# A new table of places for the same 1630 operations of a gated linear attention and channel-mix kernel

## The chip, the cores and the metric

One core of a Trainium2 chip runs the whole program. The metric is the device time of one execution in microseconds (us); lower is better. Engines named below: TensorE (PE; its weight loads are PEld), VectorE (DVE), ScalarE (ACT), GpSimd (POOL), and SyncE, whose queue (SP) issues every load and store.

## The reference

```python
# attention: B=4, H=8, S=768, D=48; per head a complex D x D state with decay a
for t in range(S):
    new_re = ar * S_re - ai * S_im
    new_im = ar * S_im + ai * S_re
    kv = np.einsum('bhd,bhe->bhde', k[:, :, t], v[:, :, t])
    S_re, S_im = (new_re + kv, new_im)
    y[:, :, t] = np.einsum('bhd,bhde->bhe', q[:, :, t], S_re)
...
# channel mix on x = y as (B, S, 384), d_ff = 1024
xk = mu_k * x + (1.0 - mu_k) * x_prev
xr = mu_r * x + (1.0 - mu_r) * x_prev
k = np.maximum(xk @ w_k, 0.0)
v = k * k @ w_v
r = 1.0 / (1.0 + np.exp(-(xr @ w_r)))
return (r * v).astype(np.float32)
```

## The kernel before

The sequence is cut into 8 units of 384 positions (4 batches, two halves each), numbered u. For each unit there are three groups of operations. **gate(u)** loads the four rows a_re, a_im, k, q (`g`), turns the decays into logarithms and angles (ScalarE: Ln, Exp, Arctan, Sin; VectorE: running sums along the positions with `tensor_tensor_scan`) and multiplies k and q by the resulting factors (`times`, L730), so that the recurrence becomes ordinary products. **attend(u)** stacks q by DMA (`stack`), transposes the keys (`tr`, L884 in unit 0 and L821 after), copies them out of PSUM (`kt`, L891/L898 and L830/L834, ScalarE), forms state updates (`up`, L923 and L853), scores (`sc`, L970 and L965) and outputs (`y`, L1011). **mix(u)** forms xk and xr, the products with w_k (called f in the table; tile `z`, L384 in unit 0, L388 after), relu and square on ScalarE (L429, L433), the products with w_v (tile `o`, L469), the products with w_r (also tile `z`), the sigmoid and the store. Unit 0 works in plain float32; from unit 1 on each operand of the mix is split in two parts (`hi`, `lo`) and each product is three passes. The weights come as ten pieces `raw` (`fetch`), are put together (`convert`: a cast on ScalarE, L535, and one VectorE instruction, L540) and later split (`split`, L559 and L562).

ScalarE holds one set of functions at a time. `act` (L248, L255) loads a set whenever the next function in program order is not in the present one: Ln and Exp are in set 6, Arctan and Sin in set 9, Sigmoid in set 2. So the order decides how many loads there are.

What sets the order of everything is the table `ORDER`: for each group (`("g", u)`, `("a", u)`, `("m", u)`, and `f`, `w`, `s` for fetch, convert and split) it gives each operation its place from 0 to 1629. `Plan.run` sorts all operations by place and emits them, and each engine then runs its own ones in that order, waiting for what it needs. SP issues its DMAs in that order too. Matmul results go to a pool of 5 PSUM tiles (`ps`, used by tr, up, sc, y and z alike; `pso` holds o), so a matmul group can wait for a tile until ScalarE or VectorE has emptied an older one.

```python
    def op_act(n, f, psum=False, **kw):
        op(f, **kw)
...
    def op_pe(cost, f, **kw):
        op(f, **kw)
...
        for i in sorted(range(len(order)), key=order.__getitem__):
            emit, after, _ = self.ops[i]
            assert after <= done
            emit()
```

The first arguments of these helpers (an operation's cost) are not read in this file.

Of the kernel before, what the change touches and what calls it, by code (L numbers as in the profile page):

```python
# [22 lines left out]
C = H * D  # L23
# [208 lines left out]
def tile_kernel(ctx, tc, gat, vt, w_all, mu, slow_g, slow_v, out):  # L232
# [29 lines left out]
    def op_act(n, f, psum=False, **kw):  # L262
        op(f, **kw)
# [970 lines left out]
```

## Time and profile before

| what | value |
|---|---|
| median of 3 runs | 428.28 us (428.24 to 428.5) |
| profiled execution, its own time | 429.0 us |
| its span (first to last instruction) | 427.0 us |
| instructions in the span | 13402 |
| TensorE busy | 375.1 us, 88% |
| VectorE busy | 327.9 us, 77% |
| ScalarE busy | 315.9 us, 74% |
| mean granted TensorE clock | 0.965 of full |

The profiled execution took 2.0 us more than its span, and lies 0.72 us above the median. Busy time is the sum of an engine's instructions; a granted clock of 1.00 is TensorE's full 2.4 GHz and 0.50 is 1.2 GHz. A row of the trace that ends in brackets gives the idle time of the engine just before it and what ended that.

### The profile page before, as it was taken

Reading aid. Unit: us, or ns where it says so; the run is one execution under the profiler, and the core shown is the slowest. Engines: PE = TensorE matmul, PEld = TensorE weight load, DVE = VectorE, ACT = ScalarE, POOL = GpSimd, SP = SyncE. Lnnn points to the kernel's source line nnn. Section 1 sums busy time; section 2 is a strip of 40 time slices with the busy share of each in tenths; the row PEclk is TensorE's granted clock in tenths of the full one; section 3 lists DMA queues with packets and bytes.
Section 4 is the critical chain, followed back from the end, with each engine's and each line's share of the span. In section 5 each row is a group of like instructions: output and inputs, shape, how many; then the busy total and the mean of one; then the engine's idle time right before and its main releaser. Section 6 shows DMA issues by size and latency. Waiting matters only on the chain.

```text
span 427.0 us, 13402 instructions
## 1 busy us (share of the span) xinstructions
PE 375.1 (88%) x5705; PEld 336.1 (79%) x5705; DVE 327.9 (77%) x528; ACT 315.9 (74%) x618; POOL 8.7 (2%) x32
## 2 busy tenths in 40 slices
PE   0047758999989999999999999999998999999991
PEld 0036734776679999999899999999997999999991
DVE  4998669889987989988989779879897684263342
ACT  6999599978977899779977896879885733361430
POOL 6000000000000000000000000000000000000000
PEclk9998659999989999999999999999999999999997
DMA  7989450464431333444331572344220340200101
GB/s 280 411 302 256 120 228 2 102 174 178 98 95 46 150 117 84 122 186 124 84 98 44 199 161 64 125 158 97 85 57 6 88 104 20 71 0 2 56 2 64
DMA packets 22996, 49.72 MB, mean 116 GB/s; under 512 B 4848, under 2 KB 16368, under 8 KB 22928
## 3 DMA queue, kind: packets, MB, share of 16 engines
q1 hardware_dynamic: 22928, 48.78, 37.2%
q8 instruction: 47, 0.77, 0.8%
q14 instruction: 21, 0.17, 0.1%
HBM read 31.06 MB, written 4.72 MB: 84 GB/s over the span
## 4 chain that ended last, share of the span: by engine, by line
PE 59%; ACT 25%; DVE 8%; issue 3%; DMA 2%; SPq 1%; ACTq 0%; DVEq 0%
PE z L388 23%; PE o L469 15%; PE y L1011 8%; PE up L853 5%; PE sc L970 3%; ACT L248 3%; ACT r L255 2%; PE z L384 2%; ACT sq L255 2%; PE tr L821 2%; ACT ph L255 2%; DVE ph L695 2%; DVE g L685 2%; ACT r L718 2%; ACT m L255 2%
## 5 line engine op out<-in xcount | busy, mean ns | idle before, releaser
L388 PE MATMUL z<-x,w 128*128 128x384 f32 x693 | 129.8, 340 | 1.0 <-ACT kt L830 1.0
L388 PEld LDWEIGHTS z<-x,w 128*128 128x128 f32 x693 | 119.3, 188 | 2.6 <-ACT kt L830 1.4
L469 PE MATMUL o<-hx,w 128*128 128x384 f32 x504 | 98.4, 342 | 0.0
L469 PEld LDWEIGHTS o<-hx,w 128*128 128x128 f32 x504 | 86.3, 188 | 1.0
L429 ACT ACTIVATE r<-z 128x384 f32<-128x384 f32 x64 | 30.1, 487 | 26.9 <-PE z L388 24.4
L730 DVE TENSOR_TENSOR g<-g,r 128x768 f32<-128x768 f32 (+1 forms) x24 | 41.6, 1754 | 8.8 <-ACT r L255 8.1
L433 ACT ACTIVATE h<-r 128x384 f32<-128x384 f32 x64 | 33.6, 525 | 4.7 <-DMA out_t<-y 3.7
L441 DVE CAST hx<-h 128x384 fp32r<-128x384 f32 x44 | 15.6, 356 | 26.0 <-PE o L469 15.4
L255 ACT ACTIVATE sq<-m 128x1152 f32<-128x1152 f32 (+1 forms) x30 | 28.0, 966 | 6.8 <-DVE m L651 3.1
L445 DVE TENSOR_TENSOR hx<-h,hx 128x384 fp32r<-128x384 f32 x56 | 30.6, 554 | 0.9 <-ACT h L433 0.2
L384 PE MATMUL z<-x,wx 128*128 128x384 f32 x66 | 24.6, 521 | 5.3 <-DVE x L347 5.3
L884 PE MATMUL tr<-ident,g 128*128 128x128 f32 x18 | 4.5, 405 | 28.1 <-DVE stat L704 27.2
L248 ACT ACT_TABLE_LOAD x22 | 28.2, 1283 | 1.2 <-PEq L1223 0.8
L364 DVE TENSOR_TENSOR x<-xm,x 128x384 fp32r<-128x384 f32 x42 | 22.6, 553 | 8.2 <-ACT x L361 7.7
L1011 PEld LDWEIGHTS y<-q,state 112*48 112x48 f32 (+1 forms) x704 | 23.5, 137 | 6.5 <-issue 4.0
L1011 PE MATMUL y<-q,state 112*48 112x64 f32 (+1 forms) x704 | 26.0, 230 | 2.6 <-ACT r L429 1.5
L361 ACT CAST x<-xm 128x384 fp32r<-128x384 f32 x42 | 21.2, 516 | 8.1 <-DVE xm L353 8.1
L853 PEld LDWEIGHTS up<-v,kt 64*64 64x64 f32 (+1 forms) x1216 | 22.5, 132 | 5.9 <-issue 1.7
L970 PEld LDWEIGHTS sc<-g 48*64 48x64 f32 x1200 | 24.2, 143 | 3.6 <-issue 2.0
L970 PE MATMUL sc<-g 48*64 48x64 f32 x1200 | 26.8, 235 | 0.0
L884 PEld LDWEIGHTS tr<-ident,g 128*128 128x128 f32 x18 | 2.9, 203 | 28.6 <-issue 27.2
L853 PE MATMUL up<-v,kt 64*64 64x48 f32 (+1 forms) x1216 | 25.2, 223 | 0.2
(89 smaller groups left out, 589.4 us busy)
## 6 DMA issues: line engine op xcount, KB each, us to landing
g<-in_gat SPq DMA_DIRECT2D x18, 768.0 KB, 5.7
raw<-in_w_all SPq DMA_DIRECT2D x9, 767.8 KB, 9.1
g<-in_gat SPq DMA_DIRECT2D x12, 384.0 KB, 8.1
v<-in_vt SPq DMA_DIRECT2D x24, 192.0 KB, 3.8
out_t<-y SPq DMA_DIRECT2D x24, 192.0 KB, 2.0
q<-g SPq DMA_DIRECT2D x84, 48.0 KB, 2.4
q<-g SPq DMA_DIRECT2D x28, 144.0 KB, 2.9
q<-g SPq DMA_DIRECT2D x40, 72.0 KB, 2.5
```

What stands on the lines that cost most here:

```text
L248: nc.scalar.add_instruction(mybir.InstLoadActFuncSet(name=nc.get_next_instruction_name(), act_func_set_id=n, engine=mybir.EngineType.Activ ...
L255: nc.scalar.activation(out=out, in_=in_, func=func, **kw)
L384: nc.tensor.matmul(z, lhsT=wx[s[0]][:, s[1]], rhs=hi[which][:, ct], start=ct == 0, stop=ct == NT - 1)
L388: nc.tensor.matmul(z, lhsT=wt[s[0]][:, part, s[1]], rhs=r[which][:, ct], start=n == 0, stop=n == 3 * NT - 1)
L429: nc.scalar.activation(out=t["r", j], in_=t["f", j], func=AF.Relu, scale=1.0 / W_SCALE)
L433: nc.scalar.activation(out=t["h", j], in_=t["r", j], func=AF.Square)
L445: nc.vector.tensor_tensor(out=t["lo", j], in0=t["h", j], in1=t["hi", j].bitcast(F32), op=ALU.subtract)
L469: nc.tensor.matmul(tiles["o", mt], lhsT=w, rhs=r, start=j == 0 and n == 0, stop=j == NJ - 1 and n == len(parts) - 1)
L730: nc.vector.tensor_tensor(out=g[:, d, 2 * i:2 * i + 2], in0=g[:, d, 2:4], in1=t["r"][:, 1 - i, d].unsqueeze(2).to_broadcast([P, k, 2, U]), ...
L853: nc.tensor.matmul(t["up", c, s][i * HR:(KR if i else HR), h * D:(h + 1) * D], lhsT=keys, rhs=V[u][c][r, h * D:(h + 1) * D], start=True, s ...
L970: nc.tensor.matmul(y, lhsT=g[:, 2 * i, q], rhs=g[:, 2 * i + 1, q], start=i == 0, stop=i == 1)
L1011: nc.tensor.matmul(t["y", team][s][rows, h // 2 - team[0], c], lhsT=lhsT[:, cols], rhs=rhs, start=(s, h % 2) not in begun, stop=stop)
```

## The change

Nearly every place in `ORDER` is new; no operation is added or taken away. The numbers handed to the helpers as costs change in seven lines as well, and these are not read when the kernel is built. A few lines of the diff:

```diff
 ORDER = {
-    ("g", 0): (0, 2, 1, 10, 13, 19, 4, 3, 23, 7, 9, 12, 15, 17, 22, 25, 27, 11, 14, 18, 21, 20, 28, 32, 37, 39, 40,
...
+    ("g", 0): (0, 1, 2, 35, 3, 6, 10, 56, 5, 7, 9, 14, 18, 11, 12, 17, 20, 15, 19, 24, 26, 22, 25, 29, 32, 42, 34, 23,
...
-        cost = 1.97 if whole else 1.62
+        cost = 1.97 if whole else 1.61
...
-                op_pe(0.1 + 0.82 * m, f0, heat=0.8, reads=k, writes=[("sc", u, team)],
+                op_pe(0.1 + 0.82 * m, f0, heat=0.68, reads=k, writes=[("sc", u, team)],
```

What it moves on the engines, at three places. First ScalarE in the gate of unit 0, in the program's first part (`sq<-m` is Exp or Ln of set 6, `ph<-ph` Arctan and `r<-r` Sin of set 9, L718 an absolute value, L535 a weight cast). Before:

```order
L255 ACTIVATE sq<-m 128x384 x6
L248 ACT_TABLE_LOAD
L255 ACTIVATE ph<-ph 128x384 x3
L535 CAST hx<-raw 128x768 x2
L718 ACTIVATE r<-r 128x384 x2
L255 ACTIVATE r<-r,half_pi 128x384 x2
L255 ACTIVATE r<-r 128x384 x2
L535 CAST hx<-raw 128x768
L718 ACTIVATE r<-r 128x384
L255 ACTIVATE r<-r,half_pi 128x384
L622 ACTIVATE m<-g 128x1152
L255 ACTIVATE r<-r 128x384
```

With the new table the same stretch reads:

```order
L255 ACTIVATE sq<-sq 128x384 x2
L248 ACT_TABLE_LOAD
L255 ACTIVATE ph<-ph 128x384 x3
L535 CAST hx<-raw 128x768
L248 ACT_TABLE_LOAD
L255 ACTIVATE sq<-m 128x384 x4
L718 ACTIVATE r<-r 128x384
L255 ACTIVATE sq<-m 128x384 x2
L535 CAST hx<-raw 128x768
L718 ACTIVATE r<-r 128x384
L248 ACT_TABLE_LOAD
L255 ACTIVATE r<-r,half_pi 128x384
```

The six Exp that feed L685 stood ahead of the Arctan and now stand behind it, so set 9 is loaded, then set 6 again, then set 9 again. Up to the keys' first copy ScalarE issues five loads instead of three; from there on the number is the same in both.

Second TensorE at the start of unit 0's mix (numbers tell tiles apart; an `x3` row of L384 is one product). Before:

```order
L384 MATMUL z_736<-x_717,wx_236 128x384 x3
L384 MATMUL z_749<-x_717,wx_206 128x384 x3
L384 MATMUL z_761<-x_717,wx_306 128x384 x3
L469 MATMUL o_774<-h_769,wx_206 128x384
L469 MATMUL o_776<-h_769,wx_206 128x384
L469 MATMUL o_778<-h_769,wx_206 128x384
L384 MATMUL z_788<-x_746,wx_727 128x384 x2
L384 MATMUL z_788<-x_746,wx_743 128x384
L384 MATMUL z_798<-x_746,wx_727 128x384 x2
L384 MATMUL z_798<-x_746,wx_743 128x384
L821 MATMUL tr_809<-ident_66,g_138 128x128 x3
```

With the new table:

```order
L384 MATMUL z_745<-x_721,wx_309 128x384 x3
L384 MATMUL z_761<-x_721,wx_180 128x384 x3
L384 MATMUL z_768<-x_721,wx_241 128x384 x3
L384 MATMUL z_782<-x_721,wx_326 128x384 x3
L469 MATMUL o_794<-h_777,wx_180 128x384
L469 MATMUL o_796<-h_777,wx_180 128x384
L469 MATMUL o_798<-h_777,wx_180 128x384
L384 MATMUL z_806<-x_757,wx_728 128x384 x2
L384 MATMUL z_806<-x_757,wx_733 128x384
L384 MATMUL z_818<-x_757,wx_728 128x384 x2
L384 MATMUL z_818<-x_757,wx_733 128x384
L821 MATMUL tr_829<-ident_66,g_141 128x128 x3
```

A fourth w_k product now stands ahead of the first group into o, and a fifth between the transposes; the second group into o moved back.

Third TensorE where the mix of unit 0 ends and the attention of unit 2 begins (`o<-h` are the last groups of unit 0, `tr`, `sc`, `up` those of unit 2). Before:

```order
L469 MATMUL o<-h,wx 128x384 x6
L821 MATMUL tr<-ident,g 128x128 x6
L469 MATMUL o<-h,wx 128x384 x3
L821 MATMUL tr<-ident,g 128x128 x3
L970 MATMUL sc<-g 64x64 x48
L821 MATMUL tr<-ident,g 128x128 x6
L853 MATMUL up<-v,kt 64x48 x2
```

With the new table:

```order
L469 MATMUL o<-h,wx 128x384 x3
L821 MATMUL tr<-ident,g 128x128 x6
L469 MATMUL o<-h,wx 128x384 x3
L821 MATMUL tr<-ident,g 128x128 x6
L469 MATMUL o<-h,wx 128x384 x3
L970 MATMUL sc<-g 64x64 x48
L821 MATMUL tr<-ident,g 128x128 x3
L853 MATMUL up<-v,kt 64x48 x2
```

Before, three of unit 2's six groups of transposes (an `x3` each) stand ahead of the scores and two right behind them; now four stand ahead, two by two between groups into o, and one behind. After the first state update the program before has a second one ahead of four mix products of unit 1 (36 matmuls of L388); with the new table those 36 come first.

## Rows read from the trace of the kernel before

**Rows 1.** The page: busy time by engine; granted TensorE clock in 40 slices, tenths.
```profile
PE 375.1 (88%) x5705; PEld 336.1 (79%) x5705; DVE 327.9 (77%) x528; ACT 315.9 (74%) x618; POOL 8.7 (2%) x32
...
PEclk9998659999989999999999999999999999999997
```

**Rows 2.** Stretches of 20 us: length, busy time (instructions) by engine, granted clock, DMA share, GB/s.
```profile
20.00:40.00 20.00, 10.77 (x258) 8.96 (x258) 18.30 (x35) 19.01 (x38) 0.00 (x0) 0.91 0.88 278
...
60.00:80.00 20.00, 18.07 (x146) 10.42 (x145) 17.35 (x23) 19.16 (x30) 0.00 (x0) 0.94 0.29 99
...
100.00:120.00 20.00, 18.36 (x155) 11.49 (x153) 18.60 (x25) 19.44 (x34) 0.00 (x0) 1.00 0.42 119
```

**Rows 3.** TensorE in order of time: start, length, engine, line, operation, count [idle before].
```profile
27.22 0.87 PE L884 MATMUL tr<-ident,g 128*128 128x128 f32 x3 [27.22 <-DVE stat L704]
...
32.95 0.90 PE L923 MATMUL up<-v,kt 64*64 64x48 f32 x48 [0.94 <-ACT kt L891]
...
53.94 0.91 PE L1011 MATMUL y<-pt,v 64*64 64x64 f32 x24
58.96 1.65 PE L384 MATMUL z<-x,wx 128*128 128x384 f32 x2 [4.12 <-DVE x L347]
60.82 6.28 PE L384 MATMUL z<-x,wx 128*128 128x384 f32 x16 [0.21 <-DVE x L347]
67.82 2.20 PE L469 MATMUL o<-h,wx 128*128 128x384 f32 x6 [0.72 <-ACT h L433]
71.01 4.11 PE L384 MATMUL z<-x,wx 128*128 128x384 f32 x12 [0.99 <-DVE x L347]
...
118.91 0.55 PE L821 MATMUL tr<-ident,g 128*128 128x128 f32 x3 [1.10 <-ACT kt L830]
120.19 0.55 PE L821 MATMUL tr<-ident,g 128*128 128x128 f32 x3 [0.74 <-ACT kt L834]
...
123.38 1.43 PE L853 MATMUL up<-v,kt 64*64 64x48 f32 x64
...
124.74 6.51 PE L388 MATMUL z<-x,w 128*128 128x384 f32 x36
...
213.26 3.39 PE L388 MATMUL z<-x,w 128*128 128x384 f32 x18 [1.05 <-ACT kt L830]
...
327.36 1.38 PE L1011 MATMUL y<-q,state 112*64 112x64 f32 x40 [1.46 <-ACT r L429]
```

**Rows 4.** Stretches of 4 us; columns as in the stretches of 20 us.
```profile
48.00:52.00 4.00, 4.00 (x98) 3.68 (x97) 3.02 (x6) 1.90 (x6) 0.00 (x0) 0.50 0.08 20
...
120.00:124.00 4.00, 3.81 (x95) 3.22 (x99) 2.40 (x5) 2.93 (x10) 0.00 (x0) 0.57 0.35 80
```

**Rows 5.** The end of the program in order of time, VectorE.
```profile
417.49 1.49 DVE L486 SCALAR_TENSOR_TENSOR y<-o,zr 128x384 f32<-128x384 f32 x3 [1.64 <-PE o L469]
```

**Rows 6.** ScalarE in order of time, first 60 us.
```profile
18.37 1.28 ACT L248 ACT_TABLE_LOAD   x1
19.66 1.35 ACT L255 ACTIVATE ph<-ph 128x384 f32<-128x384 f32 x3
...
24.07 1.10 ACT L255 ACTIVATE r<-r,half_pi 128x384 f32<-128x384 f32 x2
25.08 0.92 ACT L255 ACTIVATE r<-r 128x384 f32<-128x384 f32 x2
...
26.81 0.51 ACT L718 ACTIVATE r<-r 128x384 f32<-128x384 f32 x1
...
56.36 1.03 ACT L535 CAST hx<-raw 128x768 f16<-128x768 bf16 x1
```

**Rows 7.** VectorE in order of time: unit 0's factors, unit 1's last split.
```profile
27.23 3.56 DVE L730 TENSOR_TENSOR g<-g,r 128x768 f32<-128x768 f32 x4
...
126.42 1.02 DVE L364 TENSOR_TENSOR x<-xm,x 128x384 fp32r<-128x384 f32 x2
```

**Rows 8.** Groups by line and shape: count, busy us, mean ns, idle before with releasers.
```profile
L562 DVE TENSOR_TENSOR w<-wx,w 128x768 fp32r<-128x768 f32 x9 | 8.6, 954 | 0.4 <-ACT w L559 0.4
```

More of the change, by code (lines that the diff above doesn't have):

```diff
@@ L368, in begin @@
                     x = [("X", u, ct), ("X0", u)]
-                    op_act(U, whole_old, reads=x, writes=[("xo", u, which, ct)], uses=[part_slot[which]] + use)
+                    op_act(U + 115, whole_old, reads=x, writes=[("xo", u, which, ct)], uses=[part_slot[which]] + use)
                     op_dve(U + 60, whole_new, reads=[*x, ("xo", u, which, ct)], writes=[("xhi", u, which, ct)],
@@ L544, in convert @@
             r, k = [("raw", i + 1)], [("wx", j) for j in range(s.start, s.stop)]
-            op_act(n * C, f0, reads=r, writes=[("upper", i % HB)], uses=[sx])
+            op_act(n * C + 216, f0, reads=r, writes=[("upper", i % HB)], uses=[sx])
             op_dve(n * C, f1, reads=[*r, ("upper", i % HB)], writes=[*k, ("raw", i)], uses=[sx])
@@ L836, in f2 @@
                             in_=t["tr", c, part].rearrange("p (i j x) -> p j i x", i=NT, j=2)[:, :, :, D:])
-                    op_pe(0.41, f0, heat=0.8, reads=[("kqs" if part else "kqc", u, ct) for ct in range(NT)],
+                    op_pe(0.35, f0, heat=0.8, reads=[("kqs" if part else "kqc", u, ct) for ct in range(NT)],
                           writes=[("tr", u, c, part)], uses=[sp, g_slot[u]])
@@ L854, in up @@
                                                  lhsT=keys, rhs=V[u][c][r, h * D:(h + 1) * D], start=True, stop=True)
-                op_pe(0.535 * len(subs), up, heat=0.8, reads=[("kt", u, c, i) for i in range(4)] + [("v", u, c)],
+                op_pe(1.07, up, heat=0.8, reads=[("kt", u, c, i) for i in range(4)] + [("v", u, c)],
                       writes=[("up", u, c, s) for s in subs], uses=[*su, sk, v_slot[u][c]])
@@ L899, in f2 @@
                                        in_=t["tr", p, part].rearrange("p c (j x) -> p c j x", j=2)[:, :, :, D:])
-                    op_pe(0.41, f0, heat=0.8, reads=[("kqs" if part else "kqc", u, p)],
+                    op_pe(0.35, f0, heat=0.8, reads=[("kqs" if part else "kqc", u, p)],
                           writes=[("tr", u, p, part)], uses=[sp, g_slot[u]])
@@ L1026, in f0 @@
                                 add(h, c, s, V[u][c][r], pt(h)[r, c], c == NC - 1 and h // 2 == team[-1])
-                op_pe(0.2 + (0.19 * len(inter) + 1.05) * m / 2, f0, heat=0.8,
+                op_pe(0.2 + (0.19 * len(inter) + 1.05) * m / 2, f0, heat=0.68,
                       reads=[("pt", u, p, j) for p in team for j in range(2)] + [("v", u, c) for c in range(NC)]
```

232 rows, old and new, of the table ORDER are left out of this document.

## Prediction

> **What bounds the kernel now.** I read the page first. TensorE is busy for 375.1 of 427.0 us, ScalarE and VectorE for 316 and 328 [rows 1], so no engine is full by itself, and the clock line shows two weak places: the fourth to sixth slice (32 to 64 us) and the twelfth. The stretches of 20 us then say where TensorE is idle. Between 20 and 40 us it is busy for 10.8 us while ScalarE is busy for 19.0 [rows 2], and it begins only at 27.22 us [rows 3]. From 60 us on it is nearly full. So the program has two parts. In the first 60 us ScalarE and VectorE, which make the factors of unit 0, set the pace. After that the end is TensorE's own work plus whatever waits stand in it.
>
> Third I went through TensorE in order of time for those waits. The last product of unit 0's attention ends at 53.94 + 0.91 = 54.85 us, the mix's products run from 60.82 on (two start at 58.96), and behind that there are 0.72 and 0.99 us in unit 0's mix, 1.10 and 0.74 us ahead of transposes of unit 2, 1.05 us at 213 and 1.46 us at 327 [rows 3]. That is 6.06 us in all. One more loss is not idle time: between 120 and 124 us the granted clock is 0.57 [rows 4]. A mean of 0.57 between the levels 1.0 and 0.5 is 86% of the time at 1.2 GHz; of 3.81 us busy 3.3 ran at half speed, where 1.6 would have done. The two waits of 1.10 and 0.74 us stand just before, and TensorE was busy only 18.36 of the 20 us up to there [rows 2]. Behind the last matmul the program needs 427.0 − 417.49 = 9.5 us for multiplying, storing and its closing check [rows 5]; the new order leaves that tail alone.
>
> So a new order can win at most these 6.1 + 1.6 us behind 60 us, and whatever moves the start of the mix.
>
> **The start: later.** The new table puts the six Exp behind the Arctan, and ScalarE loads two more sets of functions. One load takes 1.28 us and the next ScalarE instruction starts 0.01 us after it ends [rows 6], so I price two at 2 × 1.285 = 2.57 us. Two Sin and one absolute value now also stand ahead of the Sin that gates the first product of k and q: 0.92 + 0.51 us less than the overlap between neighbours, 1.3 us. It ended at 25.2 us [rows 6]; now it ends at 25.2 + 2.57 + 1.3 = 29.1, or 28.1 if ScalarE's 0.99 us of idle time between 20 and 40 us [rows 2] is used up first. TensorE now starts with the scores, which need both products of VectorE, 3.56 / 4 = 0.89 us each [rows 7]. First matmul: 28.1 + 1.8 = 29.9 to 30.9, against 27.22. The keys' copies come behind the same loads, so the first state update (32.95) moves by 2.6 as well.
>
> What of that reaches the end? The unit's products wait for each other through ScalarE and VectorE, and there are waits to eat into, such as the 0.94 us before the state update [rows 3]. From 48 to 52 us TensorE is 100% busy at a granted 0.50 [rows 4], so the last part of that chain cannot shrink at that clock. I take 1.9 of the 2.57 us as arriving at the last product, 56.75. Behind it the old order has a weight cast of 1.03 us at 56.36 [rows 6] between the outputs' copies and the mix's first operand; in the new one it has gone ahead. So the mix starts at 60.82 + 1.9 − 1.0 = 61.7: **+0.9 us**. Bounds: all of the delay hidden, −1.0; all 3.4 us that the keys can be late (2.57 plus one long Exp's worth of reordering) passed on, +2.4.
>
> **Unit 0's mix: the waits go.** The first group into o waited 0.72 us for the square of a product just made, and the w_r products waited 0.99 us for VectorE's mixing [rows 3]. Now four w_k products instead of three precede it. A product takes some 2.1 us (12 matmuls in 4.11 [rows 3]), and that much time passes on ScalarE and VectorE too. Nothing else is ahead of these two, so both waits vanish: **−1.7** (between 0 and −1.7).
>
> **Unit 2's transposes: the waits and the low clock go.** Three groups stood right around the scores and waited for ScalarE to empty PSUM tiles. Now they stand two by two between groups into o, each about 2 us long, in which ScalarE makes the copies. Without 1.84 us of idle time there I let the clock stay up: 1.84 + 1.6 = **−3.4** (0 if ScalarE is as late as before).
>
> **At 213 and 327 us.** Both waits are for ScalarE to empty a PSUM tile, and both neighbourhoods are ordered anew: **−2.5** (0 to −2.5).
>
> **New waits.** A new order makes its own. The thinnest place that I found is the one where four mix products of unit 1 moved ahead of a state update. They need VectorE's last split, which ended at 126.42 + 1.02 = 127.4 [rows 7]. Nine VectorE instructions that were ahead of it are now behind, among them the last three weight splits at 0.95 us or less [rows 8], and one is new: 4.6 us by their lengths, so 122.8. TensorE would be there at 124.74 − 3.4 − 0.8 (the two terms above) − 1.4 (the update that moved behind, 1.43 at 123.38 [rows 3]) = 119.1. The gap is 3.7 us if VectorE keeps its old times, and under 1 if it moves up as TensorE does, since most of what it waits for is TensorE and ScalarE; I take 1.5. For two more places with a PSUM tile as releaser I take 0.6 each, half of what such waits cost at 213 and 327. Sum **+2.7**, bounds 0.8 and 7.6 (all that was won is given back).
>
> **Sum.** 429.0 (the profiled execution's own time) + 0.9 − 1.7 − 3.4 − 2.5 + 2.7 = 425.0. The three runs' median lies 0.72 below that execution, so I forecast **424.3 us** for the median.
>
> **A rule against the change.** The trace has a load of functions followed at once by the next instruction, 18.37 + 1.28 = 19.65 against 19.66 [rows 6]. The Trainium skill, *ScalarE: Activation LUTs*, section "What ACT_TABLE_LOAD costs", adds a drain of about 1.38 us to each switch and gives about 2.66 us in total; by that page (an estimate) two more loads would cost 5.3 us and the sum would be 2.7 us higher, 427.0. No such drain is to be seen in this row, so I keep 2.57.
>
> **Rivals.** *The start decides (slower).* ScalarE is busy 19.0, 19.2 and 19.4 of 20 us at 20, 60 and 100 us [rows 2]. If that engine and not TensorE carries the first 120 us, its 2.57 us are passed on whole, the two waits in unit 0's mix and those at 119 us stay since they end on ScalarE's copies, and only the later ones can go: 428.3 + 2.57 − 2.5 + 1.2 = 429.6. Against it: ScalarE has 0.8 us idle at 60 to 80 and 0.6 at 100 to 120 us, and at 119 us it is the order of its copies that is late. It decides if the mix starts after 64 us.
>
> *The waits only move.* PSUM has 5 tiles in both orders, and what is won at one place is given back at others: 7.6 us of old losses against as much of new, with or without 0.9 at the start: 428.3 to 429.2. For it: four of the six waits above end on ScalarE emptying a tile or handing on a result. Against it: only six stand in 356 us, so a new order of the same kind need not have as many.
>
> *No waits.* If the new order's durations fit so well that almost nothing stands in TensorE's stream behind 61 us, the new waits are 0.3 instead of 2.7 and the start is hidden: 424.3 − 2.4 − 0.9 = 421.0.
>
> *The change does nothing* can't be: the program's order differs on all engines.
>
> **Chances.** Forecast 0.53, no waits 0.15 (both faster), waits move 0.14 (nearly all of it within or about the edge of no change), the start decides 0.13 (slower), and 0.05 for the skill's price of a load (427.0, just faster). A measurement of this kernel can tell some 0.2%, 0.9 us, from no change. Faster 0.70, same 0.10, slower 0.20. The forecast's own range is 422.3 to 426.5 (0.9 either way for the start, 1.2 for the new waits); with the rivals the range is 420.3 to 429.2, which leaves out some 2 in 10.
>
> **What the changed profile would show.** Start: the first matmul at 30 us, not 27; five loads of functions before 32 us; the mix's run of products from about 61.7. Mix: no wait above 0.3 us between 63 and 77 us. Unit 2: TensorE's transposes without waits for kt, and a granted clock of 1.00 in all stretches behind 65 us. The products of L388 that open unit 1's mix wait for VectorE's L364 for about 1.5 us. Idle time of TensorE between 61 us and its last matmul of about 3 us instead of 6. I am wrong if the mix starts after 64 us, or if that idle time stays at 6 us or more.

## The result

The changed kernel's median is 421.22 us (four runs, 420.05 to 422.21) against 428.26 before (four runs); the ratio is 0.985, 95% interval 0.980 to 0.990. The forecast was 424.3 with a range of 420.3 to 429.2: the time lies inside, 3.1 us below the forecast. A second set of six runs (kernel e5 below, which ran as the changed kernel does) gave 420.9 and a ratio of 0.983. The profiled execution has a span of 420.5 us against 427.0.

### The profile page after: what moved, and what is told of

Same layout as the page of the kernel before. It is cut to its first block, busy times and chain, and to the rows that moved or that the text cites. A ratio compares the mean times of both kernels' runs of the same rounds, so it can differ in the third digit from the quotient of the medians.

```text
span 420.5 us, 13399 instructions
## 1 busy us (share of the span) xinstructions
PE 370.6 (88%) x5705; PEld 333.5 (79%) x5705; DVE 328.6 (78%) x528; ACT 316.6 (75%) x620; POOL 8.2 (2%) x32
## 4 chain that ended last, share of the span: by engine, by line
PE 63%; ACT 19%; DVE 5%; issue 4%; DVEq 0%; ACTq 0%
PE z L388 25%; PE o L469 17%; PE y L1011 8%; PE up L853 4%; PE sc L970 3%; ACT L248 2%; ACT sq L255 2%; PE tr L821 2%; ACT ph L255 1%; ACT r L255 1%; PE sc L965 1%; ACT r L429 1%; ACT h L433 1%; PE z L384 1%; ACT x L361 1%
## 5 line engine op out<-in xcount | busy, mean ns | idle before, releaser
L388 PE MATMUL z<-x,w 128*128 128x384 f32 x693 | 130.6, 340 | 0.5 <-ACT kt L834 0.4
L388 PEld LDWEIGHTS z<-x,w 128*128 128x128 f32 x693 | 119.4, 188 | 2.7 <-ACT kt L834 0.7
L469 PE MATMUL o<-hx,w 128*128 128x384 f32 x504 | 99.4, 342 | 0.0
L970 PE MATMUL sc<-g 48*64 48x64 f32 x1200 | 26.1, 228 | 30.9 <-DVE g L730 29.8
L970 PEld LDWEIGHTS sc<-g 48*64 48x64 f32 x1200 | 23.3, 137 | 34.6 <-DVE g L730 30.0
L384 PE MATMUL z<-x,wx 128*128 128x384 f32 x66 | 24.4, 524 | 5.4 <-DVE x L347 5.4
L364 DVE TENSOR_TENSOR x<-xm,x 128x384 fp32r<-128x384 f32 x42 | 23.0, 553 | 7.8 <-ACT x L361 7.6
L353 DVE SCALAR_TENSOR_TENSOR xm<-dx,mu_sb,xt 128x384 f32<-128x384 f32 x42 | 25.4, 614 | 0.6
L853 PEld LDWEIGHTS up<-v,kt 64*48 64x48 f32 (+1 forms) x1216 | 21.5, 127 | 5.1 <-issue 3.0
L384 PEld LDWEIGHTS z<-x,wx 128*128 128x128 f32 x66 | 13.4, 208 | 14.5 <-issue 7.3
L853 PE MATMUL up<-v,kt 64*64 64x48 f32 (+1 forms) x1216 | 24.0, 217 | 0.0
```

The costliest lines, as they stand in the source:

```text
L384: nc.tensor.matmul(z, lhsT=wx[s[0]][:, s[1]], rhs=hi[which][:, ct], start=ct == 0, stop=ct == NT - 1)
L388: nc.tensor.matmul(z, lhsT=wt[s[0]][:, part, s[1]], rhs=r[which][:, ct], start=n == 0, stop=n == 3 * NT - 1)
L469: nc.tensor.matmul(tiles["o", mt], lhsT=w, rhs=r, start=j == 0 and n == 0, stop=j == NJ - 1 and n == len(parts) - 1)
L853: nc.tensor.matmul(t["up", c, s][i * HR:(KR if i else HR), h * D:(h + 1) * D], lhsT=keys, rhs=V[u][c][r, h * D:(h + 1) * D], start=True, s ...
L970: nc.tensor.matmul(y, lhsT=g[:, 2 * i, q], rhs=g[:, 2 * i + 1, q], start=i == 0, stop=i == 1)
```

## The profile after

The page has 4.5 us less of TensorE's busy time than [rows 1]. In the clock line the slices of 10.5 us with a low clock are now the sixth (53 to 63 us) and the tenth (95 to 105):

```profile
PE 370.6 (88%) x5705; PEld 333.5 (79%) x5705; DVE 328.6 (78%) x528; ACT 316.6 (75%) x620; POOL 8.2 (2%) x32
...
PEclk9999969998999999999999999999999999999998
```

TensorE in order of time, columns as in [rows 3]:

```profile
29.24 0.47 PE L970 MATMUL sc<-g 48*64 48x64 f32 x2 [29.24 <-DVE g L730]
30.30 1.67 PE L970 MATMUL sc<-g 48*64 48x64 f32 x46 [0.59 <-DVE g L730]
...
43.42 0.91 PE L1011 MATMUL y<-q,state 112*64 112x64 f32 x20 [1.11 <-issue]
...
52.70 0.56 PE L1011 MATMUL y<-pt,v 64*64 64x64 f32 x24
...
58.66 9.89 PE L384 MATMUL z<-x,wx 128*128 128x384 f32 x24 [5.39 <-DVE x L347]
68.39 2.10 PE L469 MATMUL o<-h,wx 128*128 128x384 f32 x6
70.32 4.03 PE L384 MATMUL z<-x,wx 128*128 128x384 f32 x12
...
96.20 2.04 PE L1011 MATMUL y<-q,state 112*64 112x64 f32 x40 [1.87 <-ACT xt L1046]
...
120.38 3.38 PE L388 MATMUL z<-x,w 128*128 128x384 f32 x18
124.19 3.39 PE L388 MATMUL z<-x,w 128*128 128x384 f32 x18 [0.43 <-ACT kt L834]
```

The six waits of [rows 3] behind 60.8 us are gone: the group into o at 68.39 and the products at 70.32 follow without one, unit 2's transposes have none, and neither 213 nor 327 us has one. The waits over 0.3 us that are left behind the mix's start are 1.87 us at 96.20, 0.43 at 124.19 and 0.37 at 138.86. The long one is new. Stretches of 4 us, columns as in [rows 4], show what came behind it:

```profile
48.00:52.00 4.00, 3.47 (x118) 2.74 (x113) 3.13 (x6) 3.90 (x11) 0.00 (x0) 1.00 0.04 9
...
96.00:100.00 4.00, 3.80 (x89) 3.56 (x90) 3.93 (x5) 0.90 (x5) 0.00 (x0) 0.58 0.01 3
120.00:124.00 4.00, 3.76 (x31) 3.38 (x23) 3.37 (x5) 4.00 (x9) 0.00 (x0) 1.00 0.32 63
```

Behind the wait the granted clock is 0.58 for 4 us: 84% of 3.80 us at 1.2 GHz, 1.6 us lost. That is what [rows 4] had at 120 us, moved to 96. At 48 us, where [rows 4] has 0.50, the clock is now 1.00. ScalarE in order of time tells what the copy at 96 us stood behind, and how many loads the start has:

```profile
15.30 1.28 ACT L248 ACT_TABLE_LOAD   x1
16.60 1.35 ACT L255 ACTIVATE ph<-ph 128x384 f32<-128x384 f32 x3
...
93.22 1.28 ACT L248 ACT_TABLE_LOAD   x1
94.52 1.16 ACT L255 ACTIVATE ph<-ph 128x1152 f32<-128x1152 f32 x1
95.59 0.48 ACT L1046 ACTIVATE xt<-y 112x384 f32<-112x384 f32 x1
```

And VectorE's last output, which answers to [rows 5]:

```profile
412.51 1.49 DVE L486 SCALAR_TENSOR_TENSOR y<-o,zr 128x384 f32<-128x384 f32 x3 [3.25 <-PE o L469]
```

Cut at two events that both traces have, the 6.5 us of span divide without remainder:

| stretch | before, us | after, us | difference | forecast |
|---|---|---|---|---|
| start to the end of unit 0's attention | 54.85 | 53.26 | −1.6 | +1.9 |
| from there to the first y of the last output | 362.64 | 359.25 | −3.4 | −5.9 |
| from there to the end of the span | 9.51 | 7.99 | −1.5 | 0 |
| sum | 427.0 | 420.5 | −6.5 | −4.0 |

(The forecast's −5.9 is −1.0 for the weight cast, −1.7, −3.4, −2.5 and +2.7.) The total came out within the range while every stretch was off: part of that is luck.

The traces also say in what form the time went. Of the 6.5 us, 4.5 are busy time of TensorE for the same 5705 matmuls, and 2.0 are idle time. From the first matmul to the end of unit 0's attention it is busy for 22.79 us before and 19.87 after, for 578 matmuls each, at a mean granted clock of 0.77 and 1.00. So in these two executions the start gains 2.9 us of busy time and 0.7 us of waits, and loses 2.0 us by its later first matmul. The middle stretch gains 1.0 us of busy time and 2.4 us of waits.

## The experiments

Ratios are to the kernel before on the same chip; 0.001 is 0.43 us. The runs were made on more than one chip, so kernels are compared by these ratios. The changed kernel stands at 0.985 and 0.983.

| kernel | median, us | ratio, 95% interval |
|---|---|---|
| e1: Xy copies ahead of the Arctan | 419.0 | 0.977 (0.974 to 0.979) |
| e2: before, closing check freed | 424.8 | 0.991 (0.988 to 0.993) |
| e3: old start in the new table | 426.3 | 0.993 (0.990 to 0.995) |
| e4: new start in the old table | 429.3 | 1.002 (1.000 to 1.005) |
| e5: loads, no effect (changed kernel again) | 420.9 | 0.983 (0.979 to 0.987) |
| e6: before, with filler matmuls | 429.6 | 1.002 (0.998 to 1.005) |
| e7: fourth mix product put back | 422.0 | 0.987 (0.982 to 0.991) |
| e8: unit 2's attention in old order | 429.0 | 1.003 (1.000 to 1.006) |
| e9: mix's operands earlier, with e1 | 419.5 | 0.979 (0.974 to 0.983) |
| e10: two real loads more | 425.3 | 0.993 (0.990 to 0.996) |
| e11: kt copies earlier, with e1 | 420.0 | 0.980 (0.976 to 0.984) |
| e12: closing check put back behind | 423.3 | 0.989 (0.986 to 0.993) |

**e1, the wait at 96 us.** Two numbers of ("a", 1) in the new table:

```diff
-        361, 338, 354, 362, 367, 372, 301, 375, 391, 389, 371, 385, 384, 388, 396, 393, 400, 407, 402, 398, 415, 411, 410,
+        361, 338, 354, 362, 367, 372, 301, 375, 385.6, 385.5, 371, 385, 384, 388, 396, 393, 400, 407, 402, 398, 415, 411, 410,
```

> The changed kernel with unit 1's two Xy copies put ahead of gate 2's Arctan on ScalarE. Theory 1, the TensorE wait of 1.87 us at 96.20 us is for the copy that stands behind the load of functions and the Arctan, and the granted clock of 0.58 in 96 to 100 us (3.80 us busy) comes of that wait: both go, 1.87 + 1.6 = 3.4 us, 421.2 becomes 417.8, ratio 0.975 to 0.977, and the clock reads 1.00 in 96 to 100 us. Rival a, the clock falls there for another reason: only the wait goes, 419.4, ratio 0.979. Rival b, the wait moves to the next instruction that waits for a PSUM tile or for the later Arctan: 420.5 to 421.5, ratio 0.982 to 0.985.

ScalarE of this kernel now has the copy first and the load behind it:

```profile
92.69 0.47 ACT L1046 ACTIVATE xt<-y 112x384 f32<-112x384 f32 x1
...
93.87 1.28 ACT L248 ACT_TABLE_LOAD   x1
```

In its stretches of 4 us:

```profile
96.00:100.00 4.00, 4.00 (x13) 2.40 (x14) 3.57 (x5) 3.52 (x14) 0.00 (x0) 1.00 0.21 61
```

Wait and low clock are both gone. The ratio moved by 0.007 to 0.008, 2.9 to 3.6 us, against 3.4 expected; the medians moved by 2 us only. Its interval lies below both of the changed kernel's: this is the lowest ratio measured, 2.3% under the kernel before, though e9 and e11, which have the same two copies first, can't be told from it. That the wait was for this copy is shown. That the low clock comes of the wait is shown in part: e1, e9 and e11 have neither, but of the seven traces that have the wait (1.77 to 1.91 us) only five have a low clock behind it. In e7 and e3 the clock stays up. e7's rows:

```profile
96.76 1.38 PE L1011 MATMUL y<-q,state 112*64 112x64 f32 x40 [1.89 <-ACT xt L1046]
...
96.00:100.00 4.00, 3.24 (x92) 2.71 (x93) 3.93 (x6) 2.20 (x10) 0.00 (x0) 1.00 0.06 14
```

So what e1 gains over an execution like e7's is the wait alone, and how often the clock falls there isn't known from the times.

**e2 and e12, the closing check.** The old table had unit 7's copy of the last angles into `stat` (L704) at place 1628, behind the last output. e2 changes this one number of the old table, e12 puts it back in the new one:

```diff
 e2
-        1291, 1288, 1300, 1303, 1309, 1306, 1314, 1313, 1321, 1324, 1317, 1628, 1326, 1327, 1330, 1335, 1338, 1339,
+        1291, 1288, 1300, 1303, 1309, 1306, 1314, 1313, 1321, 1324, 1317, 1327.5, 1326, 1327, 1330, 1335, 1338, 1339,
 e12
-        1283, 1279, 1286, 1288, 1299, 1293, 1313, 1315, 1328, 1323, 1321, 1336, 1330, 1332, 1338, 1342, 1344, 1346,
+        1283, 1279, 1286, 1288, 1299, 1293, 1313, 1315, 1328, 1323, 1321, 1628.5, 1330, 1332, 1338, 1342, 1344, 1346,
```

> The kernel before with one number of the table changed: unit 7's copy into stat, the last instruction of the old order on VectorE (418.89 us), goes to the place behind gate 7's other VectorE work. Theory 1, the closing check's five instructions (418.89 to 420.96 us) stood behind the last output only because of that copy, and the program's tail of 9.1 us behind the last matmul becomes the 8.1 of the changed kernel: 428.3 - 1.0 = 427.3, ratio 0.9977. Rival, the stores set the end in any case: no difference, ratio 1.000. What the prediction had on record, that the tail is left alone by the new order, is then wrong by that 1.0.

> The changed kernel with one number of the table changed: unit 7's copy into stat goes behind the last output, where it stood in the old order. Theory 3: the closing check's five instructions stand behind the last output again, and the time from the last of the products into o to the end of the span grows from 8.1 to 9.1 us or more; by the second run's trace (9.1 against 6.5 us) up to 2.6 us. Ratio 0.987 to 0.990. Rival, the stores and what follows them set the end: 0.983 to 0.985, and 8.1 us as before.

VectorE at the end of e12:

```profile
411.98 1.49 DVE L486 SCALAR_TENSOR_TENSOR y<-o,zr 128x384 f32<-128x384 f32 x3 [3.33 <-PE o L469]
413.38 0.16 DVE L704 COPY stat<-ph 128x9 f32<-128x9 f32 x1
...
415.30 0.15 DVE L1128 TENSOR_SCALAR bad<-n 1x1 int32<-1x1 f32 x1 [0.37 <-PE n L1127]
```

and of e2:

```profile
415.18 1.49 DVE L486 SCALAR_TENSOR_TENSOR y<-o,zr 128x384 f32<-128x384 f32 x3 [1.64 <-PE o L469]
```

From the last output's first y to the end of the span, e12 takes 421.6 − 411.98 = 9.6 us and e2 422.1 − 415.18 = 6.9. Over all kernels of this study it is 9.5 to 9.9 us with the check behind the output (four traces) and 6.7 to 8.2 without (ten). So one number of the table is worth some 2 us, and the changed kernel had this gain in it. In the time e12 gives 0.0045 to 0.006 (1.9 to 2.6 us); its interval overlaps the changed kernel's, so it is the traces that carry this. The first expectation of 1.0 was too small, since it went by one trace near the long end of the range (7.99 of 6.7 to 8.2). e2's ratio of 0.991 (3.9 us) is more than the tail: its trace also has another start. TensorE there, in the order of before:

```profile
51.44 0.56 PE L1011 MATMUL y<-pt,v 64*64 64x64 f32 x24
56.59 1.65 PE L384 MATMUL z<-x,wx 128*128 128x384 f32 x2 [4.59 <-DVE x L347]
```

and a stretch of it:

```profile
48.00:52.00 4.00, 3.11 (x108) 2.71 (x108) 3.94 (x7) 2.68 (x10) 0.00 (x0) 1.00 0.11 27
```

Up to 300 us e2's order is that of the kernel before. Yet its attention of unit 0 ends at 52.00 instead of 54.85, at a clock of 1.00 where [rows 4] has 0.50. The same order gives two starts, 2.85 us apart. The waits in that part add up to 4.05 us against 4.82, and the 578 matmuls of it take 20.78 us of TensorE's time against 22.79, which is some 2 us for the clock.

**e3 and e4, the start alone.** The rows of `("g", 0)`, `f`, `w` and `("a", 0)` from the other table, laid into the slots that these groups have:

```diff
+START = {
+    ("g", 0): ...
+}
+slots = sorted(p for k in START for p in ORDER[k])
+rank = dict(zip(sorted(p for v in START.values() for p in v), slots))
+ORDER.update({k: tuple(rank[p] for p in v) for k, v in START.items()})
```

> The changed kernel with the old order among the instructions of gate 0, the weights' loading and unit 0's attention, in the slots that these groups have in the new table; everything else as in the changed kernel. Theory 1, the start is neutral (TensorE has done the same work at 58 us in both traces) and the gain is made behind it: 420.8 to 421.8, ratio 0.983 to 0.985. Rival a, the new start's full clock in unit 0's attention (which ended 1.6 us earlier) is part of the gain: the clock reads 0.50 again at 48 to 56 us, and the time is 1.6 to 2.3 us up, 422.8 to 423.5, ratio 0.987 to 0.989. Rival b, the prediction's term (the new start costs 0.9): 420.3, ratio 0.982.

> The kernel before with the new order among the instructions of gate 0, the weights' loading and unit 0's attention, in the slots that these groups have in the old table; everything else as before. Theory 1: no difference, ratio 0.998 to 1.002. Rival a, the new start is worth 1.6 to 2.3 us by its clock: 426.0 to 426.7, ratio 0.995 to 0.996, with a clock of 1.00 at 48 to 53 us. Rival b, the prediction's term: 429.2, ratio 1.002. In every case five loads of functions before 32 us and the first matmul at 29 to 30 us.

None of the expectations holds for e3: it loses 3 to 4 us by the ratios (5 by the medians), and not only by its attention (which ends at 55.03) but behind it. TensorE there:

```profile
63.87 2.90 PE L418 MATMUL z<-x,wx 128*128 128x384 f32 x4 [8.83 <-DVE x L381]
```

The 8.83 us of idle time (5.39 in the changed kernel) end on a chain through ScalarE, where an Exp of gate 1 stands ahead of two of the mix's operands and waits for VectorE:

```profile
60.93 1.16 ACT L289 ACTIVATE sq<-m 128x1152 f32<-128x1152 f32 x1 [1.69 <-DVE m L711]
```

e4 gains nothing. Its time is the one that rival b, the prediction's term, named (429.3, ratio 1.002), which theory 1 allows too; its attention ends at 56.44, 1.6 us later than before, at a clock of 1.00 only up to 52 us, and its mix has waits of 2.11 and 2.09 us. So the start's order and what follows it fit together in each table, and a half of one in the other tells little about the half. Neither test settles what the new start is worth.

**e5 and e10, the price of a load.** e5 called for three loads of one set in a row where one stood, e10 forced two by a Sin and an Exp of one column (its edit):

```diff
             assert after <= done
+            if places and order[i] == 85:
+                self.more()
             emit()
...
+            junk = keep.tile([P, 1], F32, name="junk")
+            plan[0].more = lambda: [act(junk, tiny, f) for f in (AF.Sin, AF.Exp)]
             plan[0].run(ORDER)
```

> The changed kernel with two more loads of functions on ScalarE, right ahead of the first Sin of gate 0 (three in a row where one stood), so that the price of two loads at that place is measured. Theory 1, the prediction's: 2 x 1.285 = 2.57 us on ScalarE, of which some 1.9 us arrives at the end of unit 0's attention and at the program's end: 423.1, ratio 0.988 to 0.990, the first matmul at 31.8 us. Rival a, the whole 2.57 us or more arrives, since the start is one chain through ScalarE: 423.8 and up, ratio 0.990 or more. Rival b, the Trainium skill's price with a drain for each switch (2 x 2.66 = 5.3 us): 426.5, ratio 0.995. Rival c, hidden in the waits of unit 0's attention: 421.2 to 421.8, ratio 0.983 to 0.985.

> The changed kernel with two more changes of the function set right ahead of the first Sin of gate 0: a Sin and an Exp of one column each, whose results nothing reads, so that two more loads must happen (of the three loads in a row of the earlier attempt only one was left in the trace). Theory 1, the prediction's price: two loads at 1.30 us from start to next start, and two small activations, some 3 us on ScalarE; the waits of unit 0's attention (3.2 us by the trace) hide about a quarter, and some 2 us arrive at the mix's start and at the end: ratio 0.988 to 0.990 (0.984 without them). Rival a, all of it arrives: 0.991 or more. Rival b, the Trainium skill's drain on top (2.66 us a switch): some 6 us on ScalarE, ratio 0.995 to 0.998, and the next instruction starts 1.4 us after a load's end. Rival c, hidden: 0.983 to 0.986.

e5's trace has the five loads of the changed kernel, not seven: of the three loads of one set without an activation between them one was left. It counts as the changed kernel measured again. e10 has them:

```profile
25.16 1.28 ACT L250 ACT_TABLE_LOAD   x1
26.46 0.20 ACT L257 ACTIVATE junk<-tiny 128x1 f32<-128x1 f32 x1
26.68 1.28 ACT L250 ACT_TABLE_LOAD   x1
27.97 0.20 ACT L257 ACTIVATE junk<-tiny 128x1 f32<-128x1 f32 x1
```

A load takes 1.30 us from its start to the next start, and 2.92 us pass from the first extra load to the instruction that it delays. The time rose by 0.008 to 0.010, 3.4 to 4.1 us: by these figures all of the 2.9 us arrives at the end and some more (its attention ends at a clock of 0.50). Rival a fits best; the intervals, 0.003 to 0.005 either way, do not quite shut out the prediction's 2 us. The Trainium skill, *ScalarE: Activation LUTs*, section "What ACT_TABLE_LOAD costs", adds a drain of about 1.38 us to a switch; no row here has one behind a load, on the path or off it: in all fourteen traces the next ScalarE instruction starts 0.01 to 0.02 us after a load's end, but for the program's first load, behind which ScalarE waits for the transfer of `g`.

**e6, the clock in unit 0's attention.** Filler matmuls in the kernel before:

```diff
+FILL = {127: 4, 138: 4, 175: 3, 204: 2}
...
+            if places and order[i] in FILL:
+                self.fill(FILL[order[i]])
...
+        def fill(n):
+            t = pso.tile([P, 512], F32, tag="o0", name="fill")[:, :P]
+            for _ in range(n):
+                nc.tensor.matmul(t, lhsT=ident, rhs=ident, start=True, stop=True)
```

> The kernel before with 13 small matmuls (128x128, into a PSUM tile that nothing reads) put into four of TensorE's waits in unit 0's attention: four ahead of the first state update, four ahead of the fourth transpose group, three ahead of the first product of queries and state, two ahead of the second. Theory 2, the granted clock in unit 0's attention falls to 0.50 because TensorE is idle there by turns, and the low clock is what moves the mix's start: the clock reads 1.00 up to 50 us in the records and the mean of every run is 0.98 or more, the mix starts 1.5 to 2.4 us earlier, 426 to 427 in all runs, ratio 0.993 to 0.996. Rival, the clock falls all the same or its fall costs nothing there: 428.3 to 429.3, ratio 1.000 to 1.002.

In the trace the clock stays at 1.00 up to 50 us, as theory 2 wants, and is 0.50 from 50 to 52. Its other sign failed: six of the twelve runs have a mean clock of 0.98 or more, not all. The time doesn't move. Two of TensorE's rows say why:

```profile
44.07 0.56 PE L926 MATMUL up<-v,kt 64*48 64x48 f32 x28 [1.87 <-issue]
...
49.82 1.57 PE L973 MATMUL sc<-g 48*64 48x64 f32 x46 [2.23 <-issue]
```

The fillers took 4.4 us where the waits that they replaced had 3.0, and waits that end on nothing the profile shows add up to 4.5 us against 1.8 before. They come in the middle of one group of like matmuls. Attention ended at 54.70, as late as before. So this execution held the clock for most of the attention but not the rest, and what the clock alone is worth at the start stays open. (The six runs at 0.98 or more have a median of 428.0 us, the others 430.2.)

**e7, the fourth product ahead of o.** Two places of ("m", 0): 278 becomes 299.5 and 294 becomes 303.5.

> The changed kernel with the fourth w_k product of unit 0's mix put back behind the first group into o and two of the w_r products (its relu with it), so that again three products stand ahead of that group. Theory 1, the prediction's term: TensorE waits again 0.7 us ahead of the group into o and some 1.0 us ahead of the products behind it, 421.2 + 1.7 = 422.9, ratio 0.988 to 0.989. Rival, the factors of the mix are ready earlier in the changed kernel anyway and the fourth product hid nothing: 421.2 to 421.6, ratio 0.983 to 0.985.

```profile
57.62 7.82 PE L384 MATMUL z<-x,wx 128*128 128x384 f32 x18 [5.39 <-DVE x L347]
65.28 2.10 PE L469 MATMUL o<-h,wx 128*128 128x384 f32 x6
69.05 6.07 PE L384 MATMUL z<-x,wx 128*128 128x384 f32 x18 [1.67 <-DVE x L347]
```

TensorE's rows show the wait back, as one of 1.67 us instead of 0.72 and 0.99. In the time it is 0.7 to 1.4 us (0.0016 to 0.003), which these intervals can't tell from nothing, nor from the 1.7 us of theory 1.

**e8, unit 2's attention.** The same lines as in e3, with `("a", 2)` alone.

> The changed kernel with the old order among the instructions of unit 2's attention, in the slots that they have in the new table; the rest as in the changed kernel. Theory 1, the prediction's term: TensorE waits again for the kt copies at its transposes (1.10 and 0.74 us) and the granted clock falls again behind them (1.6 us), 3.4 us in all, ratio 0.991 to 0.992. Rival a, the waits come back and the clock stays: 1.8 us, 0.988. Rival b, ScalarE's copies are early enough in the changed kernel in either order: 0.983 to 0.985.

It costs some 8 us, more than any theory said. TensorE waits for a copy:

```profile
119.10 0.90 PE L830 MATMUL tr<-ident,g 128*128 128x128 f32 x3 [1.64 <-ACT kt L843]
```

the clock behind it is down:

```profile
120.00:124.00 4.00, 3.67 (x70) 3.42 (x71) 2.03 (x4) 3.51 (x8) 0.00 (x0) 0.50 0.38 92
```

and the copy stood behind a load and a wide Ln on ScalarE:

```profile
116.37 1.28 ACT L257 ACT_TABLE_LOAD   x1
117.67 1.25 ACT L264 ACTIVATE m<-m,tiny 128x1152 f32<-128x1152 f32 x1
118.83 0.22 ACT L843 COPY kt<-tr 128x96 f32<-128x96 f32 x1
```

Further waits of 0.67 and 0.96 us at 128 to 131 us and 1.46 at 167 are of this kernel alone, from old places among new neighbours. The mechanism of the forecast's term is there; its size can't be read from this kernel.

**e9 and e11, further on.** With e1: gate 1's Exp and two weight conversions behind the mix's operands (e9), and a square and two kt copies earlier on ScalarE (e11):

```diff
 e9
-        240, 242, 245, 255, 261, 259, 260, 258, 263, 266, 268, 271, 269, 273, 281, 284, 287, 292, 299, 289, 297, 288,
+        240, 242, 252.5, 255, 261, 259, 260, 258, 263, 266, 268, 271, 269, 273, 281, 284, 287, 292, 299, 289, 297, 288,
-    ("w", 8): (222, 244,),
-    ("w", 9): (228, 247,),
+    ("w", 8): (222, 256.1,),
+    ("w", 9): (228, 256.2,),
 e11: ("m", 0) 453 becomes 447; ("a", 2) 506 and 508 become 502.1 and 502.2
```

> The changed kernel with the two Xy copies ahead of the Arctan (as in the first run) and three more places changed ahead of unit 0's mix: gate 1's Exp (sq0) goes behind the two last xo operands on ScalarE, and VectorE's last two weight conversions go behind the three operands of the mix. Theory: TensorE's 5.39 us of idle time ahead of the mix end on that chain, where the Exp (1.05 us) and the conversions (1.60 us) stand in the way: the mix starts 1.0 to 1.4 us earlier and keeps it, 419.0 - 1.2 = 417.8, ratio 0.973 to 0.975. Rival a, the weights' conversions or gate 1 are then late and the gain is given back in unit 0's mix or unit 1's attention: 419.0 to 419.5, ratio 0.976 to 0.978.

> The changed kernel with the two Xy copies ahead of the Arctan and three more places on ScalarE: unit 0's last square goes ahead of two kt copies of unit 2, and two more kt copies go ahead of a weight cast. Theory: the two waits that the first run's trace has left (0.57 us at 111.5 for the square, 0.47 us at 121.0 for a kt copy) go, and TensorE has no wait over 0.3 us between the mix's start and its last matmul: 1.0 us less, ratio 0.973 to 0.975. Rival, they move to the next tile: 0.976 to 0.978.

e9's TensorE:

```profile
58.09 10.73 PE L384 MATMUL z<-x,wx 128*128 128x384 f32 x24 [4.15 <-DVE x L347]
```

The idle time is shorter by the 1.24 us that was expected, but the same 24 matmuls take 10.73 us instead of 9.89, since more of them run at 1.2 GHz: from the attention's end to the end of these 24, e9 takes 14.89 us and the changed kernel 15.29, so 0.40 of the 1.24 is left. In e11 the two waits are 0.19 and none, and its trace has one of 1.63 us (on nothing shown) in unit 0's attention. Neither time can be told from e1's.

## Why the prediction was right, and where it wasn't

**What bounds the kernel** was read rightly: behind the mix's start the end is TensorE's work plus the waits in it, and e1, e7 and e8 move the end, or TensorE's stream, through single waits there.

**The start.** Predicted: attention ends 1.9 us later. It ended 1.6 us earlier in the profiled execution. What was counted is near: five loads, two matmuls at 29.24 and the rest of their group at 30.30 (29.9 to 30.9 said). The step that failed is the one that took the 0.50 clock at 48 us for a fixed floor: e2 shows that the same order ends 2.85 us earlier in an execution whose clock holds. The other step there, a quarter of the loads' delay eaten by waits, finds no support in e10, but it erred the other way. What the new order by itself costs or gains stays open: e2's 52.00 and the 54.85 of before lie as far apart as any effect in question, and eight traces with the new start lie between 51.8 and 54.9. What I missed is that the clock holds in some executions and not in others. Of 58 runs of the kernel before, 14 had a mean granted clock of 0.98 or more, with a median of 426.5 us, and 44 less, with 429.0. All ten runs of the changed kernel had 0.981 to 0.988. At like clock the change is 426.5 − 420.9 = 5.6 us, and about 2 us of the 7 to 8 between the medians come with the steadier start. That is a correlation, of a mean over the whole program, and two things stand against it: e4 has the new start and mean clocks of 0.971 to 0.982, and e6 held the clock for most of the attention and gained nothing. So the cause isn't settled.

**Unit 0's mix** (−1.7): right; the waits are gone, and e7 brings back 1.67 us. **The weight cast** (−1.0): 0.6 of it by the forecast's own mark: from the attention's end to the run of products it was 5.97 us and is 5.40. But the two matmuls that stood ahead of that run are now in it, so that TensorE idles 5.39 us in one piece instead of 4.12 and 0.21. **Unit 2** (−3.4) and **213 and 327 us** (−2.5): the trace shows the waits at both places and the low clock of unit 2 gone; e8 supports the first, the second was read from the trace only.

**New waits** (+2.7): the mis-sized term. It was 1.87 + 0.43 + 0.37 of waits and 1.6 of clock, 4.3 us, within the bounds of 0.8 to 7.6, and at another place. VectorE's L364 kept nobody waiting; the wait was for a copy on ScalarE behind a load and an Arctan, which e1 shows. I priced PSUM waits without the low clock that can follow one.

**The tail** (0): wrong, some −2 us (e12). The sentence that the new order leaves the tail alone was not looked up: the old table's 1628 among numbers near 1300 (e2's diff) was there to be seen.

So the number was right because the start and the tail came out 5 us better than said, and the middle 2.5 us worse. "No waits" named 421.0, the time that came, for a reason that did not: TensorE still waits 2.7 us. "The start decides" is refuted by the mix starting at 58.66. "The waits only move" came true in part, with 4.3 us of new losses for 7.6 of old. (Two readings under the rivals were off: five of the six waits end on ScalarE, not four, and the one of 0.99 us in unit 0's mix ends on VectorE.)

## What to carry to other kernels

Look at what stands on ScalarE ahead of the copy that empties a PSUM tile: the long wait at 96 us, that of e8, and before the change those at 118.91 and 213.26 us each had 2.3 to 2.5 us of wide functions, or one and a load, ahead of the copy. In e1 moving two copies ahead of them took the wait away; the longest that its trace then has behind the mix's start is 0.57 us. ScalarE before the change, ahead of 118.91 and of 213.26 us:

```profile
115.80 1.28 ACT L248 ACT_TABLE_LOAD   x1
117.09 1.26 ACT L255 ACTIVATE m<-m,tiny 128x1152 f32<-128x1152 f32 x1
...
210.38 1.17 ACT L647 ACTIVATE sq<-ph 128x1152 f32<-128x1152 f32 x1
...
211.68 1.17 ACT L255 ACTIVATE sq<-sq 128x1152 f32<-128x1152 f32 x1
```

Price such a wait with a low clock that may follow it, and ask the trace whether it does. It cost 1.6 us again at 96 us and at 119 us, but behind the same wait in e3 and e7, and behind the waits of 1.05 and 1.46 us at 213 and 327 us before the change, the clock stayed at 1.00. And ask of any order what its last instruction on each engine holds up: here a 0.16 us copy kept the whole closing check behind the output, worth some 2 us.

## What the hardware did that I had not expected

TensorE waits of 0.2 to 2.2 us that end on no semaphore ("issue") stand in unit 0's attention in every trace, at other instructions in each: 1.80 us at 44.48 before, 1.11 at 43.42 after, 2.23 at 49.82 in e6. They come where hundreds of small matmuls follow each other. The DMA engines are busy in several of them (a share of 0.85 in the one before the change) but not in all (0.04 in the 2.23 us of e6); the DMA view of 38 to 52 us after the change has instruction packets among them:

```profile
q8 instruction: 3, 0.05, 1.5%
```

The Trainium skill, *Runtime: NRT & Kernel Launch*, section "Instruction fetch mechanics", says that an engine's instructions are fetched in blocks by its own DMA queue and that the cost is mostly hidden. If these waits are such fetches, and no run here shows that they are, it isn't hidden in this part. The same order ended unit 0's attention anywhere from 51.8 to 54.9 us (eight traces with the new start's order), so a change of under 3 us in the start can't be judged by one trace.
